# Product of r with state and values as 32 matmuls on four quarters of the array; every PSUM bank handed out by need, and emptied first

## The chip, the cores and the metric

One core of one Trainium2 chip. The metric is the time of one execution in device microseconds. In the trace, PE is TensorE (matmuls), PEld its weight loads, DVE is VectorE, ACT ScalarE, POOL GpSimd and SP the engine that issues most DMAs.

## The reference: a recurrent attention, then a routed expert layer

For each of 4 batches and 8 heads a 40 x 40 state runs over 768 steps, and 3072 tokens of 320 then go through eight experts:

```python
for t in range(S):                                   # S = 768
    y[:, :, t] = einsum('bhd,bhde->bhe', rt, state)
    Sa = einsum('bhde,bhe->bhd', state, at)
    state = state * wt[:, :, None, :] - einsum('bhd,bhe->bhde', Sa, bt) \
          + einsum('bhd,bhe->bhde', vt, kt)
x = y as (3072, 320)                                 # then: score, argmax of 8 experts
out = x + gate * (relu(x @ w1[e]) @ w2[e])           # for tokens whose skip score is > 0
```

All arithmetic is fp32 (the expert products are split into two fp32r parts).

## The kernel before

**Chunks.** The 768 steps are cut into 24 chunks c of 32 steps. The 32 (batch, head) pairs are held as two halves x = 0 and 1; one half's 16 pairs lie on partitions 0 to 39 and 64 to 103. For each chunk and half the work is a chain of small products, each of 16 (or 32) matmuls with 40, 72 or 104 moving columns, with a copy out of PSUM behind each:

- `rs(c,x)`, on even chunks only: r of two chunks (64 columns of `rrt`) with the tile `SV`, which holds the state and the values side by side. One matmul per pair, in two PSUM banks. DVE then multiplies the state rows by `D` into `R1t` (two instructions), ACT copies the value rows into `R1t` (four).
- `ux(c,x)` reads the finished `R1t` block; ACT copies the result to `UX`. `uq(c,x)` multiplies by the inverse in `TB`; four ACT copies put it back into `R1t`, and POOL masks it (`R1t<-R1t,mc`).
- `sst(c,x)` gives the next state: on even chunks 16 matmuls of 72 columns and four ACT copies; on odd chunks two products of 40 columns, one of which ACT copies to `SV`, where the next `rs` reads it.
- `yy(c,0)` and `yy(c,1)` write the outputs of a chunk into one bank (`py`), which DVE empties into `XS` with one multiply. The tile stays in its bank from the first to the second.

Around the chain stand `m1` (products for the inverse, ACT and DVE empty them), `kbt` and `wtt` (transposes), `tinv` (the inverse itself: DVE steps on `px` and `M`, over four chunks), scans on DVE, the routing of finished tokens (`xpose`, `score`, `place`), and DMAs.

**The plan.** From c = 1 to c = 21 no instruction is issued at once. `Rec.call` records each as a task with a cost from `Rec.cost` (one task may be a whole product). At c = 22 `Rec.flush` works out their dependences, gives each task a key (its place in the program less the length of the longest chain of tasks behind it), lets `Rec.plan` place them on the engines by a simulated clock, and issues them in that order. Each engine then works through its own list strictly in order; semaphores hold it where an operand is not ready. All recorded instructions carry one line number in the trace, L230; the others have L117. So groups are told apart by tiles.

**The banks.** The core has eight PSUM banks. Five of them (`pq`, `pc` twice, `ps` twice) are in `rec.banks`: `plan` gives a recorded tile any of these that is free (`ps` only to `ps` tiles and to the oldest tile without a bank), whatever its name in the source. `px` (two) and `py` (one) are outside the pool: `px` serves `tinv`, `py` serves `yy`. In `deps` tasks on different engines that touch a `py` or `px` tile are kept in program order. An instruction that empties a bank has no precedence over others.

`plan` also has a model of TensorE's program fetch: it counts each recorded matmul as four instructions, and lets 256 instructions begin no sooner than 3.6 us after the 256 before.

Of the kernel before, what the change touches and what calls it, by code (L numbers as in the profile page):

```python
# [14 lines left out]
PSUM = bass.MemoryType.PSUM  # L15
# [41 lines left out]
class Rec:  # L57
# [32 lines left out]
    def use(s,ap):  # L90
        n=ap.name
        if 'DRAM' in str(ap.space).upper(): return [(('d',n),15,1)] if n.startswith('xg') else []
        if n[:2] in ('py','px'): n=(n[:2],)
        q,m=s.mask(ap)
        return [(('v',s.own[n]) if n in s.banks else n if isinstance(n,tuple) else ('s',n),q,m)]
    def cost(s,e,op,w,r,a):
        sz=lambda x: int(np.prod([d[1] for d in list(x.ap)[1:]])) if len(list(x.ap))>1 else 1
        n=max(sz(x) for x in (w[:1]+r[:1]))
        if 'dma' in op:
            by=4*n*min(128,w[0].ap[0][1])  # L100
            if 'ind' in op:
                s.ni+=1; return (3.6 if s.ni%2 else 1.05),2.6
            return 0.6,2.2+by/1.7e5
        if e=='P':
            if op=='transpose': return 0.145,0
            o=sz(w[0]); m,k=w[0].ap[0][1],r[0].ap[0][1]
            return (0.03+0.0006*o if m in (40,64) or k==40 and m>64 else 0.04 if k<128 and o<70 else 0.0575 if k<128 else 0.03+0.00026*o),0
        if e=='A': return 0.15+0.00085*n,0
        if e=='G': return (0.08+n*0.0008 if op=='memset' else 0.18 if op=='tensor_copy' else 0.25+0.0021*n),0
        ps=any('PSUM' in str(x.space).upper() for x in w+r)  # L110
        if op=='tensor_tensor_scan': return 0.1+0.00217*n,0
        if op=='transpose': return 0.16+0.00115*n*(1 if n<1000 else 1.4),0
        if op=='memset': return 0.08+0.0003*n,0
        if op=='tensor_tensor': return 0.14+0.00105*n*(1 if ps else 1.6),0
        return 0.16+0.00105*n,0
    def call(s,e,op,fn,a,k):
# [17 lines left out]
    def deps(s):  # L134
        acc={}
        for t in s.tasks: t.p,t.n,t.al=set(),[],set()
        for i,t in enumerate(s.tasks):
            for wr,L in ((0,t.R),(1,t.W)):
                u={}
                for n,q,m in L: u[n,q]=u.get((n,q),0)|m  # L140
                for (n,q),m in u.items():
                    if n[0]=='v': t.al.add(n[1])
                    h=acc.setdefault(n,[])
                    for j,w2,q2,m2 in h:
                        if j!=i and ((wr or w2) and q&q2 and m&m2 or n[0] in ('v','py','px') and s.tasks[j].e!=t.e and (n[0]!='v' or 'P' in (s.tasks[j].e,t.e))): t.p.add(j)
                    if wr and n[0] in 'sd': h[:]=[x for x in h if not (x[0]!=i and x[2]|q==q and x[3]|m==m)]
                    h.append((i,wr,q,m))
        for i,t in enumerate(s.tasks):
            for j in t.p: s.tasks[j].n.append(i)
        for t in reversed(s.tasks):  # L150
            t.up=t.d*s.PW+max([s.tasks[j].up+t.lat+(s.HOP if s.tasks[j].e!=t.e else 0) for j in t.n],default=0)
    def plan(s,keep=False):
# [59 lines left out]
                if not users[o]:  # L212
                    at[bank[o]]=last[o]
        s.st,s.fin,s.bank_of,s.en,s.span=st,fin,bank,en,max(fin)
    LET=1.0; FAR=1.0; ALT=1.0; FILL=None
    def keys(s):

        w=max(sum(t.d for t in s.tasks if t.e==e) for e in 'VAGP')/len(s.tasks)
        s.key=[i*w-s.FAR*t.up for i,t in enumerate(s.tasks)]
    def flush(s):  # L220
        s.on=False
        s.deps(); s.keys(); s.plan()
# [40 lines left out]
def attn(ctx,tc,i,m,out):  # L263
# [3 lines left out]
    rec=m.rec; nc=rec.shim  # L267
# [1 line left out]
    pp=m.pp  # L269
    bk=lambda n,k: [pp.tile([128,512],F32,name=f"{n}{q}") for q in range(k)]  # L270
    PQ,PC,PS,PY,PX=bk("pq",1),bk("pc",2),bk("ps",2),bk("py",1),bk("px",2)
    rec.banks={t.name:t for t in PQ+PC+PS}; rec.rest=[t.name for t in PS]
    ps_c,ps_s,ps_p=(Ring(t,rec) for t in (PC,PS,PQ)); ps_y,ps_x=Ring(PY),Ring(PX); m.ps=ps_p
    V,A,G,TE,SP=nc.vector,nc.scalar,nc.gpsimd,nc.tensor,nc.sync
    NC=4*NPH; NH=2*NPH
    SE=(V,G)[SCAN_POOL]
# [230 lines left out]
    def rs(c,x):  # L507

        if c>=NC or c%2: return
        rr=rrt[c//2].rearrange("p (b h) t -> p b h t",b=2)  # L510
        R=R1[x][c%NR1]; e=slice(eo[x],eo[x]+40); n=(128,104)[x]
        RV=[ps_c.tile([128,8,64],F32,tag="pc",name="psRV") for _ in range(2)]
        with rec.one():
            for hh in range(4):
                for b in (0,2,1,3):
                    s=slice(64*(b//2),64*(b//2)+40); v=(b%2)*4+hh
                    TE.matmul(RV[b//2][0:n,v,:],SV[x][s,v,0:n],rr[s,b%2,2*hh+x,:],start=True,stop=True)
        for bh in range(2):
            V.tensor_tensor(R[e,8*bh:8*bh+8,40:104],RV[bh][e],H[c//2]['D'][e,8*bh:8*bh+8].unsqueeze(2).broadcast_to([40,8,64]),ALU.mult)
        for bh in range(2):  # L520
            A.copy(R[ao[x]:ao[x]+32,8*bh:8*bh+8,40:104],RV[bh][ao[x]:ao[x]+32])
        for bh in range(2):
            A.copy(R1[x][1][ao[x]:ao[x]+32,8*bh:8*bh+8,40:72],RV[bh][uo[x]:uo[x]+32,:,0:32])
        load_vv(c//2+1,x)
# [69 lines left out]
    if 1:  # L594

        with tc.manual_schedule(engines={ET.Pool}):
# [72 lines left out]
            ps_p=r4  # L669
# [488 lines left out]
```

## Time and profile before

| | us |
|---|---|
| median of 3 runs (626.65 to 632.09) | 629.97 |
| the profiled execution, its own time | 625.79 |
| its span, first to last instruction | 624.0 |
| mean granted clock of TensorE, share of full speed | 0.879 |

| busy over the span | us | share |
|---|---|---|
| PE | 504.8 | 81% |
| PEld | 425.0 | 68% |
| DVE | 454.9 | 73% |
| ACT | 365.1 | 59% |
| POOL | 310.5 | 50% |

The shares are averages over stages with different limits; PE is counted busy while any matmul is in flight. One fp32 matmul of the source leaves two MATMUL and two LDWEIGHTS records, so x32 in a row is 16 matmuls of the source. [...] A bracket behind a row gives the idle time of that engine just before it and what released it.

### The profile page before, as it was taken

What the parts mean: (1) busy time and instruction counts of PE and PEld (TensorE: products, weight loads), DVE (VectorE), ACT (ScalarE), POOL (GpSimd) and SP (SyncE); (2) the same over time, 40 slices, a digit from 0 to 9 for tenths busy, and PEclk for the clock granted to TensorE, in tenths of its full rate; (3) what the DMA queues carried; (4) which work ended last, traced back from release to release, by engine and by line L of the source; (5) the groups of instructions that cost most, each with busy time, mean ns of one, the idle gap of its engine ahead of it and who ended that gap; (6) DMA issues with size and microseconds to landing.
All of it is one profiled execution on the core that took longest, in us unless ns stands there. A gap on an engine that the chain in (4) does not pass through costs nothing. (4 is left out here: it accounts for less than half of the span.)

```text
span 624.0 us, 27220 instructions
## 1 busy us (share of the span) xinstructions
PE 504.8 (81%) x11748; PEld 425.0 (68%) x11748; DVE 454.9 (73%) x1088; ACT 365.1 (59%) x858; POOL 310.5 (50%) x225
## 2 busy tenths in 40 slices
PE   5775748787785888778787898888787999999995
PEld 2543437676674776667666686766675699999995
DVE  8998957885888668876868759575463458888871
ACT  6471646665864658556675768577655355554540
POOL 5471874446446754275553913321222156666661
PEclk9686767868995889859798989799867999999998
DMA  7873197235452454335443345443566587766100
GB/s 193 209 195 92 36 211 186 71 86 129 111 144 78 103 148 117 93 86 137 120 121 99 92 111 142 117 109 80 140 158 176 154 228 227 232 220 197 51 27 24
DMA packets 80688, 81.93 MB, mean 131 GB/s; under 512 B 49041, under 2 KB 68062, under 8 KB 80099
## 3 DMA queue, kind: packets, MB, share of 16 engines
q1 hardware_dynamic: 78643, 76.35, 46.2%
q0 software_dynamic: 1920, 3.79, 1.7%
q8 instruction: 94, 1.54, 1.0%
q14 instruction: 31, 0.25, 0.1%
HBM read 62.69 MB, written 13.15 MB: 122 GB/s over the span
## 5 line engine op out<-in xcount | busy, mean ns | idle before, releaser
L230 POOL TENSOR_TENSOR R1t<-R1t,mc 64x512 f32<-64x512 f32 x42 | 60.6, 1444 | 90.4 <-ACT R1t L230 64.3
L230 ACT COPY R1t<-pc 32x288 f32<-32x288 f32 (+4 forms) x155 | 67.1, 435 | 28.7 <-PE pc L230 23.7
L117 POOL TENSOR_TENSOR WL<-WR,WH 128x1280 fp32r<-128x1280 f32 (+1 forms) x21 | 58.0, 2789 | 7.1 <-ACT WH L117 7.0
L230 DVE TENSOR_TENSOR px<-px,M 128x168 f32<-128x168 f32 (+10 forms) x240 | 58.2, 267 | 2.1
L230 DVE TENSOR_TENSOR M<-M,px 128x168 f32<-128x168 f32 (+10 forms) x240 | 55.1, 255 | 2.3
L230 ACT COPY R1t<-ps 40x288 f32<-40x288 f32 (+3 forms) x86 | 37.4, 435 | 23.8 <-PE ps L230 16.2
L230 ACT COPY R1t<-pq 32x512 f32<-32x512 f32 (+3 forms) x84 | 37.4, 445 | 16.8 <-PE pq L230 9.8
L230 POOL TENSOR_TENSOR WR<-WR,M 104x1024 f32<-104x1024 f32 x14 | 34.0, 2441 | 18.4 <-DMA WR<-kb 11.8
L117 ACT CAST WH<-WR 128x1024 fp32r<-128x1024 f32 (+1 forms) x35 | 39.7, 1133 | 0.0
L230 PE MATMUL ps<-R1t,L2t 128*40 128x40 f32 (+1 forms) x800 | 34.0, 238 | 6.6 <-ACT R1t L230 6.4
L117 POOL DMA_INDIRECT out<-ro,ti x16 | 15.7, 982 | 45.6 <-DVE ro L117 10.4
L117 DVE CAST ti<-xe 128x2 int32<-128x2 f32 x8 | 37.4, 4673 | 0.2
L230 DVE TENSOR_TENSOR_SCAN M<-M 104x1041 f32<-104x1041 f32 (+1 forms) x14 | 35.4, 2529 | 0.8 <-ACT WE L230 0.7
L117 ACT ACTIVATE hH<-pc 128x512 fp32r<-128x512 f32 x21 | 12.6, 598 | 39.1 <-PE pc L117 39.1
L230 PEld LDWEIGHTS ps<-R1t,L2t 128*40 128x40 f32 x800 | 27.3, 135 | 11.2 <-ACT R1t L230 8.4
L230 PE MATMUL pc<-rrt,SV 40*104 40x64 f32 (+1 forms) x272 | 29.9, 285 | 5.0 <-DVE base L230 2.3
L117 PE MATMUL pc<-xH,WH 128*128 128x256 f32 x126 | 32.5, 283 | 0.0
L230 PEld LDWEIGHTS pc<-rrt,SV 40*104 40x104 f32 (+1 forms) x272 | 27.9, 197 | 5.8 <-DVE base L230 2.5
L230 POOL TENSOR_TENSOR M<-M,mc 128x256 f32<-128x256 f32 x18 | 16.9, 945 | 30.1 <-DVE M L230 17.6
L230 POOL DMA_INDIRECT xg<-XS,ix x18 | 21.6, 1201 | 19.8 <-DMA xg<-XS,ix 6.2
L117 DVE TENSOR_TENSOR WL<-WR,WH 128x1024 fp32r<-128x1024 f32 (+1 forms) x19 | 23.8, 1254 | 9.7 <-ACT WH L117 9.2
L230 PE MATMUL py<-L2t,R1t 128*32 128x40 f32 x1344 | 23.7, 218 | 7.7 <-DVE XS L230 4.3
(385 smaller groups left out, 1614.7 us busy)
## 6 DMA issues: line engine op xcount, KB each, us to landing
WR<-w SPq DMA_DIRECT2D x16, 640.0 KB
WR<-w SPq DMA_DIRECT2D x16, 512.0 KB
L2t<-SCR SPq DMA_DIRECT2D x40, 160.0 KB
WR<-kb SPq DMA_DIRECT2D x32, 160.0 KB
WR<-w SPq DMA_DIRECT2D x16, 256.0 KB
R1t<-vt SPq DMA_DIRECT2D x48, 80.0 KB
SV<-vv SPq DMA_DIRECT2D x48, 80.0 KB
out<-XS SPq DMA_DIRECT2D x24, 160.0 KB
```

Source lines behind the costliest of these rows:

```text
L117: if not s.on: return fn(*a,**k)
L230: for fn,a,k,own in s.tasks[i].calls: (fn if s.en[i]==s.tasks[i].e else s.nc.vector.tensor_copy)(*[at(x,own) for x in a],**{n:at(x,own) fo ...
```

## The change

Four parts. (1) In `rs`, each matmul is split in two by output rows: one with the 40 stationary columns of the state, one with the 64 that hold the values, each on its own half of the array's columns; the two partition halves of the operands already alternate. So 32 matmuls visit four quarters in turn, where 16 matmuls alternated between two halves. The copies behind them are as before. (2) `px` and `py` join the pool, eight banks in all, and lose the special ordering. (3) A task of an engine other than PE that touches a PSUM tile which PE also uses gets its key lowered by `DRAIN` = 30, so it goes ahead of others on its engine. (4) Other constants in `Rec.cost`.

```diff
     def use(s,ap):
-        if n[:2] in ('py','px'): n=(n[:2],)
-        return [(('v',s.own[n]) if n in s.banks else n if isinstance(n,tuple) else ('s',n),q,m)]
+        return [(('v',s.own[n]) if n in s.banks else ('s',n),q,m)]
     def cost(s,e,op,w,r,a):
-            if op=='transpose': return 0.145,0
+            if op=='transpose': return 0.0014*r[0].ap[0][1],0
-            return (0.03+0.0006*o if m in (40,64) or k==40 and m>64 else 0.04 if k<128 and o<70 else 0.0575 if k<128 else 0.03+0.00026*o),0
-        if e=='A': return 0.15+0.00085*n,0
+            return (0.042 if k==40 and m>=40 else 0.041 if o<17 else 0.036+0.00072*o if m==40 else 0.0146+0.00041*o if m==32 else 0.03+0.00165*o)*1.05,0
+        if e=='A': return (0.95 if op=='activation' and n==512 else 0.38 if n==128 else 0.15+0.00085*n),0
...
-        if op=='transpose': return 0.16+0.00115*n*(1 if n<1000 else 1.4),0
+        if op=='transpose': return 0.16+0.00105*n*(1.7 if 'TB' in w[0].name else 1),0
+        if op=='tensor_tensor' and ps and n>300 and not any('PSUM' in str(x.space).upper() for x in r): return 0.14+0.00177*n,0
...
-                        if j!=i and ((wr or w2) and q&q2 and m&m2 or n[0] in ('v','py','px') and s.tasks[j].e!=t.e and (n[0]!='v' or 'P' in (s.tasks[j].e,t.e))): t.p.add(j)
+                        if j!=i and ((wr or w2) and q&q2 and m&m2 or n[0]=='v' and s.tasks[j].e!=t.e and 'P' in (s.tasks[j].e,t.e)): t.p.add(j)
...
+    DRAIN=30.0
     def keys(s):
-        s.key=[i*w-s.FAR*t.up for i,t in enumerate(s.tasks)]
+        pe=set()
+        for t in s.tasks:
+            if t.e=='P': pe|=t.al
+        s.key=[i*w-s.FAR*t.up-(s.DRAIN if t.e!='P' and t.al&pe else 0) for i,t in enumerate(s.tasks)]
...
-    rec.banks={t.name:t for t in PQ+PC+PS}
-    ps_y,ps_x=Ring(PY),Ring(PX)
+    rec.banks={t.name:t for t in PQ+PC+PS+PX+PY}
+    ps_y,ps_x=Ring(PY,rec),Ring(PX,rec)
...
     def rs(c,x):
-        e=slice(eo[x],eo[x]+40); n=(128,104)[x]
+        e=slice(eo[x],eo[x]+40); g=slice(ao[x],ao[x]+64)
-                    TE.matmul(RV[b//2][0:n,v,:],SV[x][s,v,0:n],rr[s,b%2,2*hh+x,:],start=True,stop=True)
+                    for q in (e,g): TE.matmul(RV[b//2][q,v,:],SV[x][s,v,q],rr[s,b%2,2*hh+x,:],start=True,stop=True)
```

## Rows read from the trace of the kernel before

**Rows 1.** Busy time of each engine in five stages, in us from the span's start: columns are the stage, its length, busy time (x instructions) of each engine, the mean granted clock, the busy share of the DMA engines and their GB/s. The recorded part is 74.3 to 445.

```profile
74.30:88.00 13.70, 2.59 (x133) 2.25 (x132) 6.07 (x9) 2.50 (x10) 10.97 (x15) 0.73 0.69 173
88.00:445.00 357.00, 290.00 (x8734) 243.31 (x8734) 264.94 (x818) 240.28 (x608) 175.70 (x136) 0.88 0.45 115
445.00:480.00 35.00, 26.16 (x738) 22.02 (x730) 17.55 (x35) 19.43 (x51) 8.02 (x7) 0.75 0.60 160
480.00:604.00 124.00, 121.90 (x1000) 115.50 (x990) 95.65 (x133) 60.76 (x89) 71.69 (x35) 0.99 0.57 172
604.00:624.00 20.00, 12.82 (x97) 12.55 (x95) 4.91 (x10) 2.39 (x4) 3.92 (x5) 0.89 0.08 27
```

**Rows 2.** The same table for four stretches of 17.5 us inside the loop.

```profile
192.50:210.00 17.50, 12.74 (x277) 11.03 (x273) 12.76 (x39) 8.94 (x22) 10.04 (x11) 0.59 0.33 90
210.00:227.50 17.50, 15.08 (x558) 12.74 (x554) 11.78 (x15) 10.53 (x29) 12.47 (x11) 1.00 0.59 148
...
262.50:280.00 17.50, 11.78 (x264) 10.29 (x260) 13.87 (x46) 9.81 (x25) 11.86 (x12) 0.61 0.26 73
280.00:297.50 17.50, 15.28 (x524) 12.89 (x522) 10.92 (x18) 11.19 (x31) 9.97 (x10) 1.00 0.53 136
```

**Rows 3.** From the timeline of PE, the twelve longest of its waits in the loop whose releaser read a bank of the kind that the waiting matmul writes: start, length, instruction, count, and the wait in brackets.

```profile
121.56 0.40 PE L230 MATMUL pc<-rrt,SV 40*104 40x64 f32 x1 [2.18 <-DVE TB L230]
...
150.08 0.32 PE L230 MATMUL pq<-rrt,SV 40*128 40x64 f32 x1 [1.36 <-DVE M L230]
...
183.80 0.42 PE L230 MATMUL pc<-WR,L1t 128*32 128x64 f32 x14 [1.33 <-ACT R1t L230]
196.14 0.42 PE L230 MATMUL py<-L2t,R1t 128*32 128x40 f32 x11 [2.88 <-DVE XS L230]
202.31 0.44 PE L230 MATMUL ps<-WR,L1t 128*32 128x64 f32 x8 [1.53 <-ACT R1t L230]
228.82 0.30 PE L230 MATMUL pq<-rrt,SV 40*104 40x64 f32 x1 [1.22 <-DVE M L230]
...
250.04 0.37 PE L230 MATMUL pc<-WR 128*32 128x64 f32 x12 [1.45 <-ACT SCR L230]
257.88 0.43 PE L230 MATMUL ps<-mc,XS 128*128 128x128 f32 x1 [1.93 <-DVE R1t L230]
269.79 0.43 PE L230 MATMUL pc<-rrt,SV 40*104 40x64 f32 x1 [2.30 <-DVE base L230]
274.61 0.44 PE L230 MATMUL ps<-WR 128*32 128x64 f32 x8 [1.10 <-DVE R1t L230]
337.40 0.42 PE L230 MATMUL ps<-WR,L1t 128*32 128x64 f32 x14 [1.08 <-ACT xT L230]
388.78 0.32 PE L230 MATMUL py<-L2t,R1t 128*32 128x40 f32 x13 [1.00 <-DVE XS L230]
```

**Rows 4.** From the table of waits in the loop: who waited for whom, us in total, how often, the longest. "issue" is time in which the engine waited for nothing that the profile shows.

```profile
PE ps L230 <- ACT R1t L230: 9.6, 16, 1.6
PE pc L230 <- issue: 7.9, 9, 2.7
PE pc L230 <- ACT R1t L230: 7.6, 13, 1.3
```

**Rows 5.** All matmuls of r with state and values (instructions that touch `rrt`): in the loop and in the stretch behind it; columns are busy time (x records) of PE and PEld, then clock and DMA.

```profile
88.00:445.00 357.00, 46.41 (x640) 42.48 (x640) 0.88 0.45 115
445.00:480.00 35.00, 5.49 (x64) 5.03 (x64) 0.75 0.60 160
```

**Rows 6.** Bursts of matmuls in the timeline of PE, all at the full clock: start, length from the first record to the end of the last, stationary shape, moving shape, records. The first is r with the values in the prologue (16 matmuls of the source with 32 stationary columns, on four quarters of the array), the second and third the product of the loop for x = 0 and for x = 1 (16 of the source), the fourth a product of `sst` with 40 stationary columns on two column halves (8 of the source).

```profile
31.40 0.65 PE L117 MATMUL pq<-rrt,SV 40*32 40x64 f32 x32
219.24 2.16 PE L230 MATMUL pc<-rrt,SV 40*128 40x64 f32 x32
334.15 1.68 PE L230 MATMUL pc<-rrt,SV 40*104 40x64 f32 x32 [0.23 <-ACT UX L230]
438.07 0.51 PE L230 MATMUL ps<-R1t,L2t 128*40 128x40 f32 x16
```

**Rows 7.** Groups by tile: the state's multiply on DVE and the value copies on ACT that empty the product (x busy us, mean ns), and one of the 128-column copies.

```profile
L230 DVE TENSOR_TENSOR R1t<-pc,D 40x512 f32<-40x512 f32 x17 | 11.7, 691 | 17.7 <-PE pc L230 12.5 <-ACT R1t L230 2.7 <-PE pq L230 2.3
L230 ACT COPY M<-pc 128x128 f32<-128x128 f32 x18 | 6.9, 384 | 4.0 <-PE pc L230 3.7
L230 ACT COPY R1t<-pc 32x512 f32<-32x512 f32 x17 | 9.6, 575 | 11.6 <-PE pc L230 9.4 <-POOL R1t L230 1.4 <-PE pq L230 0.6
L230 ACT COPY R1t<-pc 32x256 f32<-32x256 f32 x17 | 6.0, 363 | 0.9 <-PE py L230 0.6
```

**Rows 8.** DVE's timeline around the wait at 269.79: a scan, and the read of `base`; then the inverse when it is put into `TB`.

```profile
264.37 3.38 DVE L230 TENSOR_TENSOR_SCAN M<-M 104x1040 f32<-104x1040 f32 x1
...
269.58 0.15 DVE L230 TENSOR_TENSOR base<-pc,base 128x8 f32<-128x8 f32 x1
...
280.63 1.98 DVE L230 STREAM_TRANSPOSE TB<-M 128x1024 f32<-128x1024 f32 x1
```

**Rows 9.** PE's timeline where the chunk begins that first reads this inverse.

```profile
298.69 0.36 PE L230 MATMUL pq<-UX,TB 32*32 32x104 f32 x5
```

**Rows 10.** The DMA queues: the one that carries TensorE's program, packets and MB; and PE waits in the timeline that only "issue" ended.

```profile
q8 instruction: 94, 1.54, 1.0%
...
96.03 0.38 PE L230 MATMUL pc<-UX,TB 32*32 32x72 f32 x11 [2.66 <-issue]
...
226.47 0.38 PE L230 MATMUL pc<-UX,TB 32*32 32x104 f32 x7 [0.58 <-issue]
...
296.95 0.39 PE L230 MATMUL pc<-R1t,L1t 128*32 128x104 f32 x8 [1.18 <-issue]
```

## What the change should do to the time

> **What bounds the kernel now.** I read the stages first. Behind 480 us the experts keep TensorE busy for 121.90 of 124 us; the change doesn't touch that. The recorded loop fills 357 us, and there no engine is full: PE 81%, DVE 74%, ACT 67% [rows 1]. So the loop is bound by PE together with what PE waits for. The second view cuts it into equal stretches: two of them execute 558 and 524 matmul records at the full clock, two others only 277 and 264, at a mean granted clock of 0.59 and 0.61 [rows 2]. The slow ones are where PE stood waiting, and where the clock then fell to its lower level. Third, the waits of PE one by one, to see which are for an operand and which for a bank. Twelve have a releaser that was reading a bank of the kind the waiting matmul writes; they sum to 19.4 us [rows 3]. PE's waits for ACT's copies to `R1t` are the largest groups by name, 9.6 and 7.6 us, and part of these are for operands [rows 4]. Last, the product of r itself: 46.41 us of PE in the loop for 20 products (640 records of 32), 2.32 us each, and 5.49 us for the two behind it [rows 5].
>
> **The product of r.** At the full clock one takes 2.16 us for x = 0 and 1.68 us for x = 1 [rows 6]. Both stream 64 columns through 16 matmuls and differ only in their stationary columns, 128 against 104: the ratio of the times is 1.29, that of the columns 1.23. So the loading of the weights sets their pace now, not the streaming. The mean at the full clock is 1.92 us; the 2.32 us measured is 1.21 times that, from products that ran partly at the lower clock or with a wait inside.
>
> The new form, 32 matmuls on four quarters, is not in this trace. Its nearest row has the same `rrt` and `SV`, the same 64 moving columns and four quarters in turn, with 32 stationary columns: 16 matmuls in 0.65 us [rows 6]. Twice that is 1.30 us, one end. The other end: if matmuls that share half the array's rows or columns don't overlap, only two run at a time. The `sst` product with 40 stationary columns on two halves takes 0.51 us for 8, so 32 would take 2.04 us, a loss of 0.12 us against 1.92. I take 1.30, the row that differs least. With the same factor 1.21 this is 1.57 us, and 20 products cost 31.4 in place of 46.41 us: 15.0 us of PE less. If the lower clock goes too it is 46.41 - 26.0 = 20.4; at the bad end 20 x 2.47 = 49.4, 3 us more.
>
> Not all of that reaches the end. What frees PE ahead of a waiting instruction is worth nothing. A product is emptied by two DVE multiplies (691 ns each, 1.4 us) and four ACT copies (2 x 575 and 2 x 363 ns, 1.9 us) [rows 7], unchanged, and `ux` waits for all six. But the product stands on the chain from `SV` to `ux`, and it blocks PE for the other half's work; both speak for a gain. I count half, 7.5 us. Behind the loop two products save 5.49 - 2 x 1.57 = 2.3 us, half of it 1 us.
>
> **The banks.** Three more banks come into the pool, those of `px` for as long as no inverse is in work and `py` when no output is open, and the emptying instruction goes first on its engine. Which of the 19.4 us this removes can be followed at one place. At 269.79 the product waited 2.30 us for DVE to read `base` out of its bank; DVE read it at 269.58, after a scan from 264.37 to 267.75 and a train of steps of the inverse [rows 8]. An instruction under way isn't broken off, so going first would have put the read at 267.75, and 1.8 of 2.3 us go. A free bank would take all of it. At 196.14 and 388.78 `yy` waited 2.88 and 1.00 us for its only bank to be read into `XS` [rows 3]; a second bank takes both. Against it: a matmul let in earlier soon meets the next wait, for ACT's copy of its operand. Of 19.4 us I count 8, some 40%; the ends are 0 and all 19.4.
>
> **What goes first pushes something back.** On DVE that is the inverse, in whose place evacuations now run. It was in `TB` at 282.61 [rows 8], and the first matmul that reads it began at 298.69 [rows 9]: 16 us of cover. I cost the delay at nothing. If the cover were gone, every microsecond would stand on the chain, five times (one inverse for four chunks). `px` as a pooled tile could also hold two banks that the chain needs, but they are the two that it held before. The relaxed order of `px` and `py` adds no instruction.
>
> **The costs in the plan** change no instruction, only the order. The old constant gave the product 16 x 0.0684 = 1.09 us, where the rows have 1.68 and 2.16; a 128-column ACT copy had 0.26 and now has 0.38, where the row has 384 ns [rows 7]. An order planned by nearer costs should wait less, but nothing here prices it. I take zero, with 9.6 us on either side, the whole of the largest wait of PE for ACT in rows 4, as what an order can win or lose.
>
> **Sum.** 7.5 + 1 + 8 = 16.5 us against the profiled execution's own 625.79: 609.3. That execution lies 4.2 us under the median of the runs, 629.97, so the forecast is 613.5, taken as 614.
>
> **Rivals.**
>
> *Everything is gained* (slack on PE is used at once, the clock stays up): 15.0 + 2.3 + 19.4 = 36.7 us, 593; less the scan that can't be broken off and similar remnants, 598. For it: the fast stretches of rows 2 show that the loop can run twice as many matmuls in the same time. Against it: DVE has 265 us of its own work in the loop and ACT 240 [rows 1].
>
> *Emptying takes over.* The product falls below the 1.9 us that ACT needs to empty it, PE then waits for ACT where it waited for the bank, and the gains of both parts shrink to the 1 us behind the loop and some 3 of the banks: 626. For it: PE's waits for ACT's `R1t` copies are the largest groups already [rows 4]. Against it: ACT is at 67%, and a bank can now be had elsewhere. [...]
>
> *The quarters don't overlap*, so the change doesn't do what it says: 3 us lost, 8 gained, 5 in all: 625. The prologue burst speaks against it.
>
> *TensorE's program runs dry, and the kernel is slower.* The split adds 16 matmuls to 22 products, four instructions each: 20 x 64 = 1280 in the loop, on 17468 [rows 1], 7.3%. The program comes in 94 packets [rows 10]; the page counts 23496 matmul and load records, so 250 a packet. The densest stretch has 558 + 554 in 17.5 us [rows 2], 15.7 ns each, 3.9 us a packet. Where PE is at that pace, the time follows the count of instructions and not their length: 1280 x 15.7 ns = 20 us if all of them fell there, 13 if two thirds do, while the shorter product buys nothing; with 3 us from the banks this is 640. It decides where a packet's worth of work takes less than 3.9 us. For it: PE stood still for "issue", which could be such a wait, for 7.9 us [rows 4], once for 2.66 us [rows 10]. Against it: the stretches that hold the slow products run at half the pace. [...]
>
> **How the numbers follow.** The forecast 0.47 (606 to 623), everything gained 0.14 (598), emptying takes over 0.17 (626), no overlap 0.08 (625), program dry 0.14 (640). One per cent of 629.97 is 6.3 us, and that is about what a measurement of this kernel can tell from no change: its three runs lie within 5.4 us. Below 623.7 lie the forecast but for a sliver, and all of the first rival: 0.61. Within one per cent lie the second and third and that sliver: 0.26. Above 636.3 lies most of the last: 0.13. The range leaves out 0.2: half of the first rival, most of the last: 598 to 637.
>
> **What would show it.** The product's matmuls in the loop should sum to 26 to 32 us of PE in place of 46.41, twice as many records, each burst near 1.3 us; 40 or more says that the quarters don't overlap. The `yy` waits for `XS` and the waits of the product for `base` and `M` should be gone, and the clock of the loop above 0.88. Emptying takes over if PE's waits for `R1t` grow by what the bank waits lose. The program runs dry if "issue" grows past 15 us and falls inside bursts. An inverse that reaches `TB` less than a few us before its first reader would make the step on cover wrong; so would an ordering in which PE's waits are as long as now, at other places.

## The result: 609.62 us, and the profile after

| | before | after |
|---|---|---|
| median, us | 631.03 (626.65 to 632.68) | 609.62 (604.67 to 616.53) |
| ratio after / before | | 0.9645, 95% interval 0.9537 to 0.9753 |
| the profiled execution, us | 625.79 | 604.67 |
| its span, us | 624.0 | 602.5 |
| mean granted clock | 0.879 | 0.908 |

The change made the kernel 3.5% faster; 614 was forecast, in a range of 598 to 637. The time is right. Two of the steps that lead to it are not: one gave nothing that the runs can tell, and another gave more than it was counted for.

Some executions are 1.5 to 2.2% longer than the fastest of the same kernel (of the kernel after, one took 616.53 us at a mean granted clock of 0.89, the fastest 604.67 at 0.908); medians in this text are over all executions, while ratios leave such ones out. The kernel before was timed again beside every run (medians of 626.98 to 631.03 us), and a ratio is to that. So kernels are compared by their ratios, of which 1% is some 6.3 us; where only medians are given, the text says so.

From the page of the kernel after: busy time of the engines, and TensorE's program queue (packets, MB, share).

```profile
PE 477.5 (79%) x12452; PEld 397.2 (66%) x12452; DVE 463.2 (77%) x1100; ACT 359.3 (60%) x846; POOL 305.3 (51%) x225
...
q8 instruction: 100, 1.64, 1.2%
```

PE is busy 27 us less than before and has 704 more matmul records; its program has grown by six packets [rows 10]. The stages of the kernel after, as in rows 1 (stage, length, busy time and instructions of PE, PEld, DVE, ACT, POOL, then clock and DMA):

```profile
73.50:86.50 13.00, 1.03 (x46) 0.70 (x35) 5.69 (x7) 2.43 (x8) 10.90 (x14) 0.71 0.63 157
86.50:421.50 335.00, 269.84 (x9398) 220.56 (x9398) 277.42 (x830) 235.35 (x603) 171.88 (x136) 0.92 0.50 129
421.50:460.00 38.50, 24.08 (x806) 19.72 (x803) 18.39 (x37) 20.03 (x53) 8.34 (x7) 0.75 0.53 144
460.00:582.00 122.00, 120.26 (x971) 114.53 (x972) 92.06 (x134) 60.26 (x87) 71.79 (x35) 0.99 0.56 163
```

The same borders in the work lie in the kernel before at 87, 445, 481 and 604 us:

```profile
87.00:445.00 358.00, 291.00 (x8762) 244.14 (x8766) 265.94 (x819) 240.40 (x609) 176.51 (x136) 0.88 0.45 116
445.00:481.00 36.00, 27.16 (x750) 22.77 (x739) 17.61 (x36) 20.37 (x54) 8.02 (x7) 0.75 0.59 157
```

The whole gain is in the recorded loop: 358 to 335 us, 23 less. The stretch behind it is 2.5 us longer. The experts are as before.

The product of r in the loop and behind it, after (the view of rows 5: busy time and records of PE and PEld, clock, DMA):

```profile
86.50:421.50 335.00, 29.34 (x1280) 25.49 (x1280) 0.92 0.50 129
421.50:460.00 38.50, 3.88 (x128) 3.24 (x128) 0.75 0.53 144
```

It takes 29.34 us of PE where it took 46.41 [rows 5]; the forecast was 31.4. The quarters do overlap. One product at the full clock, first and last lines of its burst in PE's timeline, where its records go to two banks by turns:

```profile
329.85 0.27 PE L233 MATMUL px<-rrt,SV 40*40 40x64 f32 x2
...
330.79 0.22 PE L233 MATMUL py<-rrt,SV 40*64 40x64 f32 x1
```

From 329.85 to 331.01 it is 1.16 us, where rows 6 have 2.16 and 1.68 and the forecast had 1.30. But other products of the loop have holes:

```profile
112.66 0.27 PE L233 MATMUL pq<-rrt,SV 40*64 40x64 f32 x1 [0.66 <-issue]
...
248.74 0.27 PE L233 MATMUL px<-rrt,SV 40*40 40x64 f32 x2 [0.45 <-issue]
...
263.20 0.32 PE L233 MATMUL pq<-rrt,SV 40*40 40x64 f32 x3 [0.25 <-issue]
```

In the middle of a burst all operands are there and the banks are open. These waits have no releaser on any engine. The table of PE's waits from 100 to 421 us shows how many there are (who waited for whom: us in total, times, the longest; it starts at 100 us to leave out the wait of some 12 us with which the loop begins in both kernels):

```profile
PE px L233 <- issue: 5.8, 9, 1.2
PE pc L233 <- issue: 5.7, 10, 1.7
PE pq L233 <- issue: 3.8, 8, 0.8
PE py L233 <- issue: 3.2, 4, 2.2
...
PE ps L233 <- issue: 2.4, 5, 1.1
```

They sum to 20.9 us. The same stretch of the kernel before has 6.5:

```profile
PE pc L230 <- issue: 4.5, 6, 1.2
PE pq L230 <- issue: 0.9, 2, 0.5
PE py L230 <- issue: 0.8, 2, 0.6
PE ps L230 <- issue: 0.3, 1, 0.3
```

Waits for ACT's copies to `R1t` went the other way, from 20.1 to 8.0, those for DVE's writes of `R1t` from 8.7 to 4.0, and those for `base` from 2.6 to none. All waits of PE together are 58.3 us after and 58.9 before (62.4 up to the end of its loop at 445): little of the gain is that PE waits less. Bank waits went and "issue" took their place. By the stages above, 21 of the 23 us are busy time of PE (291.00 to 269.84), 17 of them the product; the granted clock of the loop rose from 0.88 to 0.92.

What most of the "issue" waits are can be read from the trace. Number all records of TensorE, its matmuls, its weight loads and the semaphore instructions between them, in order of start, and look for holes of more than 0.15 us from one start to the next. They pile up at one place of each 256 records: before record 193, 449, 705 and so on, the same in both kernels and in the runs below. From 100 us to the end of the loop the kernel after has 71 such places; 28 of them have a hole, 23.1 us in all, while no other place of the 256 has more than 5 holes or 3.9 us. The kernel before has 67 places, 15 holes and 10.5 us. Of the "issue" waits 15.3 of 20.9 us end at such a place after (the one at 112.66 is among them, the other two above are not), and 6.6 of 7.2 before. The program comes in 100 packets for 24904 matmuls and loads, so about 250 a packet, and 26 of the 28 holes end 1.1 to 1.8 us after such a packet has landed. No two packets in the loop begin less than 3.38 us apart (3.26 in the kernel before; the model in `plan` has 3.6). So I read these holes as TensorE waiting for the next block of its program. Below they are called block holes.

### The profile page after: what moved, and what is told of

Its sections match the earlier page's. It is cut to its first block, busy times and chain, and to the rows that moved or that the text cites. A ratio compares the mean times of both kernels' runs of the same rounds, so it can differ in the third digit from the quotient of the medians.

```text
span 602.5 us, 28644 instructions
## 1 busy us (share of the span) xinstructions
PE 477.5 (79%) x12452; PEld 397.2 (66%) x12452; DVE 463.2 (77%) x1100; ACT 359.3 (60%) x846; POOL 305.3 (51%) x225
## 5 line engine op out<-in xcount | busy, mean ns | idle before, releaser
L233 ACT COPY R1t<-pc 32x288 f32<-32x288 f32 (+4 forms) x121 | 52.7, 437 | 20.7 <-PE pc L233 12.5
L233 ACT COPY R1t<-px 32x288 f32<-32x288 f32 (+4 forms) x91 | 40.3, 443 | 16.0 <-PE px L233 6.1
L117 DVE TENSOR_TENSOR WL<-WR,WH 128x1024 fp32r<-128x1024 f32 (+1 forms) x19 | 23.8, 1254 | 12.5 <-ACT WH L117 11.9
L233 POOL DMA_INDIRECT xg<-XS,ix x18 | 18.4, 1022 | 28.1 <-DVE XS L233 16.8
L233 ACT COPY R1t<-py 32x416 f32<-32x416 f32 (+4 forms) x56 | 25.3, 451 | 8.0 <-PE py L233 4.6
L117 PE MATMUL ps<-WH,hH 128*128 128x320 f32 x88 | 27.6, 314 | 0.0
L117 PE MATMUL pc<-xH,WL 128*128 128x256 f32 x126 | 27.3, 281 | 0.0
L117 PE MATMUL ps<-WL,hH 128*128 128x320 f32 x88 | 27.2, 309 | 0.0
L117 PE MATMUL ps<-WH,hL 128*128 128x320 f32 x88 | 27.2, 309 | 0.0
L233 DVE TENSOR_TENSOR pc<-pc,M 128x48 f32<-128x48 f32 (+20 forms) x96 | 25.8, 269 | 1.8
L117 ACT COPY R1t<-pc 32x416 f32<-32x416 f32 (+3 forms) x36 | 15.6, 440 | 18.0 <-DVE R1t L117 11.6
L117 PE MATMUL ps<-mc 128*128 128x512 f32 x34 | 22.8, 778 | 4.4 <-DMA mc<-mc 2.9
```

Source lines behind the costliest of these rows:

```text
L117: if not s.on: return fn(*a,**k)
L233: for fn,a,k,own in s.tasks[i].calls: (fn if s.en[i]==s.tasks[i].e else s.nc.vector.tensor_copy)(*[at(x,own) for x in a],**{n:at(x,own) fo ...
```

## The experiments

The theory behind the forecast had two halves: the shorter product is worth half of its PE time, and the banks with the emptying first are worth a little more than that. The main rival was that TensorE's program cannot follow, so that the time goes by the count of instructions. "Pinned" kernels keep the exact order of issue of the kernel that they are compared with: the edited task is given the cost and the instruction count that the plan had for it, so only what is issued differs.

**The new product alone, in the order of before** (pinned).

```diff
-                    TE.matmul(RV[b//2][0:n,v,:],SV[x][s,v,0:n],rr[s,b%2,2*hh+x,:],start=True,stop=True)
+                    for q in (e,g): TE.matmul(RV[b//2][q,v,:],SV[x][s,v,q],rr[s,b%2,2*hh+x,:],start=True,stop=True)
...
+        rec.pin(0.03+0.0006*64,16,64)
```

> The order, the banks and the precedence of the kernel before (its plan is kept: the product's task keeps its old cost and its old count of instructions), and only the product executes as 32 matmuls on four quarters. Measured so far: before 631.0, after 609.6 us. If the shorter product pays as the prediction counted (half of some 15 to 18 us of PE, and 1 behind the loop): 619 to 624 us, product's PE time in the loop 28 to 32 us in place of 46.4. If the gain came from the order and the banks alone, or the added instructions eat the product's gain: 627 to 632 us, and in the second case PE's issue waits in the loop grow from 10 us by 5 or more.

Measured: 629.14 us, ratio 1.0034 (1.0001 to 1.0067). The product between 88 and 421 us, in the kernel before and in this one (whose profiled execution took 634.73 us):

```profile
88.00:421.00 333.00, 43.96 (x598) 40.30 (x600) 0.87 0.45 116
88.00:421.00 333.00, 29.57 (x1216) 25.15 (x1216) 0.86 0.46 116
```

PE's waits for "issue" rose from 9.1 to 20.8 us (from 100 us on, 6.5 to 18.4). The matmuls are 14 us shorter and the kernel is not: the block holes of the loop rose from 10.5 to 24.7 us, by as much.

**The old product in the order of after** (pinned).

```diff
-                    for q in (e,g): TE.matmul(RV[b//2][q,v,:],SV[x][s,v,q],rr[s,b%2,2*hh+x,:],start=True,stop=True)
+                    TE.matmul(RV[b//2][0:n,v,:],SV[x][s,v,0:n],rr[s,b%2,2*hh+x,:],start=True,stop=True)
...
+        rec.pin(0.042*1.05,32,128)
```

> The converse: order, banks and costs of the kernel after (plan kept), but the product executes as 16 matmuls as before, 1280 instructions fewer in the loop. If the product pays on its own: 617 to 624 us against 609.6. If the program of TensorE is what now binds, the longer product is paid back by fewer issue waits: these fall from 25 us in the loop towards 15, and the time is 606 to 613 us. If order alone made the gain: 609 to 611.

Measured: 605.52 us, ratio 0.9681 (0.9638 to 0.9724): nearly the whole gain without the new product. By the ratios the product is worth 0.4% here, 2 us, and the intervals allow anything from 5 us lost to some 10 gained (an estimate from the two intervals). Its "issue" waits are back at 7.0 us from 100 to 421:

```profile
PE px L238 <- issue: 2.8, 3, 1.4
...
PE pq L238 <- issue: 1.5, 3, 1.0
PE py L238 <- issue: 1.5, 2, 0.8
...
PE pc L238 <- issue: 0.7, 1, 0.7
...
PE ps L238 <- issue: 0.5, 1, 0.5
```

The product runs 41.14 us here against 29.34, 14 us of "issue" have gone, and the block holes are 10.4 us in place of 23.1: in this order, too, what the split saves on PE is about what it adds in holes. In the old order it bought nothing, in its own nothing that these runs can tell.

This run shows one thing more. Its matmuls are those of the kernel before, and its loop is 30 us shorter (358 to 328):

```profile
86.50:414.50 328.00, 273.97 (x8758) 229.35 (x8758) 276.04 (x832) 235.30 (x607) 172.25 (x136) 0.93 0.52 132
```

PE is busy for 273.97 us where the same work took 291.00, at a granted clock of 0.93 in place of 0.88. The granted clock reads 1.0 or 0.5 in the traces (in the kernel before 0.50 from 189.70 to 206.77 us and 1.00 from there to 230.66); 0.5 was granted for 48 us of this loop and for 89 us of the one before. So more than half of what the new order gains in the loop is busy time of PE, which goes with the higher clock, and the rest is time in which PE stood idle. Whether the fewer waits brought the clock up isn't tested.

**No precedence for emptying.**

```diff
-    LET=1.0; FAR=1.0; DRAIN=30.0; ALT=1.0; FILL=None
+    LET=1.0; FAR=1.0; DRAIN=0.0; ALT=1.0; FILL=None
```

> The kernel after with DRAIN = 0: eight banks, new product and new costs, but nothing that empties PSUM goes ahead; the plan is made anew. If the precedence carries a good part of the bank gain: 614 to 622 us, and waits of PE for DVE reads of a bank (base, XS, M) come back above 1 us each. If eight banks are enough without it: 606 to 612.

Measured: 629.02 us, ratio 1.0043 (1.0004 to 1.0082): the gain is gone, 4.0% by the ratios. PE's waits of 100 to 421 us:

```profile
PE pq L233 <- DVE base L233: 10.1, 1, 10.1
PE ps L233 <- DVE R1t L233: 6.9, 5, 1.8
...
PE px L233 <- DVE R1t L233: 5.7, 2, 3.1
...
PE pq L233 <- DVE R1t L233: 2.7, 1, 2.7
```

One wait alone costs 10 us. The timelines of PE and of DVE at that place:

```profile
183.57 0.48 PE L233 MATMUL ps<-rrt,SV 40*40 40x64 f32 x4
194.13 0.37 PE L233 MATMUL pq<-rrt,SV 40*40 40x64 f32 x2 [10.08 <-DVE base L233]
```

```profile
183.23 2.32 DVE L233 TENSOR_TENSOR_SCAN M<-M 104x1041 f32<-104x1041 f32 x1
...
186.43 1.43 DVE L233 TENSOR_SCALAR D<-M 104x16 f32<-104x16 f32 x1
...
188.37 2.31 DVE L233 TENSOR_TENSOR_SCAN M<-M 104x1040 f32<-104x1040 f32 x1
...
193.76 0.24 DVE L233 TENSOR_TENSOR M<-M,px 128x84 f32<-128x84 f32 x1
193.92 0.16 DVE L233 TENSOR_TENSOR base<-pq,base 128x8 f32<-128x8 f32 x1
```

The product stands in its own middle, with its second bank still unread: DVE does two scans and 24 other instructions, most of them steps of the inverse, before the read of `base`, 0.16 us long, that gives the bank back. It is the event of [rows 8], more than four times as long. Eight banks do not help against it: once the plan has given the product that bank, it waits.

**Precedence alone, on the kernel before.**

```diff
-    LET=1.0; FAR=1.0; ALT=1.0; FILL=None
+    LET=1.0; FAR=1.0; DRAIN=30.0; ALT=1.0; FILL=None
     def keys(s):
...
-        s.key=[i*w-s.FAR*t.up for i,t in enumerate(s.tasks)]
+        pe=set()
+        for t in s.tasks:
+            if t.e=='P': pe|=t.al
+        s.key=[i*w-s.FAR*t.up-(s.DRAIN if t.e!='P' and t.al&pe else 0) for i,t in enumerate(s.tasks)]
```

> The kernel before with the one line of precedence (DRAIN = 30), nothing else: five banks by need, old product, old costs. If the precedence alone makes the gain, as the run without it (629.0) suggests: 604 to 614 us, against 627 to 631 for before. If it needs the nearer costs or the three banks: 618 to 630.

Measured: 621.29 us, ratio 0.9877 (0.9832 to 0.9923). Faster by 1.2%, about 7 us by medians: a real part, but not the whole.

**`px` and `py` outside the pool, the rest of the change in place.**

```diff
-    rec.banks={t.name:t for t in PQ+PC+PS+PX+PY}
+    rec.banks={t.name:t for t in PQ+PC+PS}
-    ps_y,ps_x=Ring(PY,rec),Ring(PX,rec)
+    ps_y,ps_x=Ring(PY),Ring(PX)
```

(the last lines shortened; the lines of `use` and `deps` as they were before)

> The kernel after with px and py outside the pool again (five banks by need, old ordering of px and py); product, precedence and costs as after; the plan is made anew. If the three banks carry a good part: 614 to 622 us and yy waits for XS again. If precedence and product make the gain: 606 to 612.

Measured: 609.49 us, ratio 0.9738 (0.9692 to 0.9784). The median is that of the kernel after, but the kernel before was 4 us faster beside this run, and the ratio is 0.9% worse, some 6 us; the two intervals overlap. So with the precedence in place the three banks are worth 6 us at best guess and by these intervals anything from nothing to some 13; the runs don't settle it.

**Precedence and the new costs, five banks, old product.**

```diff
...
+            return (0.042 if k==40 and m>=40 else 0.041 if o<17 else 0.036+0.00072*o if m==40 else 0.0146+0.00041*o if m==32 else 0.03+0.00165*o)*1.05,0
...
+        rec.pin(0.042*1.05,32,64)
```

> The kernel before with the precedence and the new cost constants only (the old product priced at the 1.41 us of after): five banks, old product. If these two parts, which issue no instruction differently, make the whole gain: 602 to 612 us. If the three banks or the product carry some of it: 613 to 622.

Measured: 619.45 us, no ratio: three executions took 619.35 to 620.3 us, one 609.16, so each of the two expectations has its execution. This run decides nothing.

**Instructions against time.** The sharpest question is whether PE in the kernel after is held by the time of its matmuls or by their number. Two kernels keep its order and add work to each of the 20 products in the loop, in front of it and into the same banks, where the product overwrites it; nothing of the computation is left out. One adds 32 tiny matmuls (2560 instructions in all), the other a single one of 320 columns over the full array (80 instructions, 17 us of PE by the trace).

```diff
+            for hh in range(4 if rec.on else 0):
+                for b in (0,2,1,3):
+                    s=slice(64*(b//2),64*(b//2)+40); v=(b%2)*4+hh
+                    for q in (0,64): TE.matmul(RV[b//2][q:q+32,v,0:8],SV[x][s,v,q:q+32],rr[s,b%2,2*hh+x,0:8],start=True,stop=True)
...
+        rec.pin(0.042*1.05,32,128)
```

```diff
+            if rec.on: TE.matmul(RV[0][:,0:5,:],m.tri,m.mc[:,0:320],start=True,stop=True)
...
+        rec.pin(0.042*1.05,32,128)
```

> The plan of the kernel after is kept; each of the 20 recorded products executes 32 further small matmuls ahead of its own (32 stationary, 8 moving columns; their results are overwritten), 2560 instructions in all, some 0.6 us of PE each, 12 in all. If the program is what binds: issue waits grow from 25 to 45 us or more, the time to 625 to 645. If only PE's time counts: 610 to 622, the issue waits as they were.

> The counterpart: the plan of the kernel after is kept; each recorded product has one further matmul of full width with 320 moving columns ahead of it (overwritten as well), four instructions, 0.55 to 0.8 us of PE each, 11 to 16 in all. If the program binds, this time lies in place of issue waits: these fall or stay, and the time is 607 to 616 us. If PE's time binds as such: 616 to 626.

Measured: 644.91 us (ratio 1.0263, 1.0214 to 1.0313) with the tiny matmuls, 607.91 (0.9628, 0.9565 to 0.9692) with the long ones. The long ones cost nothing that can be told: the ratio is that of the kernel after (0.9645) to 0.2%, with some 8 us either way by the two intervals. The tiny ones cost 35 us by medians, 13.8 ns an instruction. "issue" from 100 to 421 us rose to 35.0 us, while it is 17.5 with the long ones. Of the kernel with tiny matmuls, the busy times on its page; its loop, which now ends at 464.5 us (columns as in the stages above); and the product in it, tiny matmuls included:

```profile
PE 515.8 (80%) x13732; PEld 433.7 (67%) x13732; DVE 463.2 (72%) x1100; ACT 359.8 (56%) x846; POOL 302.3 (47%) x225
...
86.50:464.50 378.00, 306.37 (x10678) 256.64 (x10678) 272.18 (x830) 235.73 (x604) 168.14 (x136) 0.83 0.44 114
...
86.50:464.50 378.00, 47.30 (x2560) 41.46 (x2560) 0.83 0.44 114
```

So the 13.8 ns are not the price of the program alone. In this trace the loop is 43 us longer than after (335). Its block holes are 46.2 us where after has 23.1, 23 us more or 9 ns for each added instruction. The product holds PE 18 us longer (29.34 to 47.30). And all other matmuls hold it 19 us longer (240.50 to 259.07), though they are the same: the granted clock of the loop is 0.83 in place of 0.92. That PE time as such is not the price is shown by the long matmuls: they add as much of it (17 us), their block holes are as before (23.0 us), their loop runs at 0.93 and the kernel is no longer. How much of the 35 us is the lower clock, and whether the holes brought it down, these runs don't separate.

The mean pace says less. From 88 to 421 us the kernel with tiny matmuls executes 18842 records of matmuls and loads, the kernel after 18673: 17.7 and 17.8 ns each, and the kernel before comes to 20.4 ns in its loop (358 us by 17528 records, in its row above). But `p_old_order`, with as much "issue", is at 19.0 ns (17566 records), so there is no one pace that all such loops keep.

**Fewer instructions in the order of after** (pinned). In the loop the score products are issued as one matmul each where they were four on quarters, the place products as two where they were eight: 840 instructions less, and longer matmuls.

```diff
-            for q in range(4): nc.tensor.matmul(lg[32*q:32*q+32],xT[:b-a,k,32*q:32*q+32],s.wg[:b-a,k,:],start=k==0,stop=k==2)
+            for q in ((slice(0,128),) if s.rec.on else [slice(32*q,32*q+32) for q in range(4)]): nc.tensor.matmul(lg[q],xT[:b-a,k,q],s.wg[:b-a,k,:],start=k==0,stop=k==2)
...
```

(and the place products likewise)

> The order, banks and costs of the kernel after (plan kept); only the routing in the loop is written with full-width matmuls: score as 3 in place of 12, the two products of place as 1 in place of 4 each. Some 840 instructions fewer on TensorE in the loop (of some 18800), its busy time about the same. So far: after 609.6, the same order with the old product 605.5 us, PE's issue waits in the loop 25 and 8.5 us. If these waits are TensorE's program arriving late: they fall from 25 us to between 8 and 17, and the time is 598 to 606 us. If they are something that the split product does on the array: unchanged at 23 to 27 us, and 607 to 612.

Measured: 599.84 us, ratio 0.9539 (0.9498 to 0.958). "issue" from 100 us on fell from 20.9 to 10.9. The score and place products take 9 us more of PE (10.87 to 18.52 and 1.66 to 3.16 us between 88 and 421), and the kernel is some 10 us faster by medians, 7 by the ratios; the intervals overlap. It is the trade of the change's product, run backwards, but the block holes fell by less than that (23.1 to 16.6 us), so the trade alone doesn't explain a gain.

**The same routing with the old product** (pinned; beside the lines of `fewer_instr`).

```diff
-                    for q in (e,g): TE.matmul(RV[b//2][q,v,:],SV[x][s,v,q],rr[s,b%2,2*hh+x,:],start=True,stop=True)
+                    TE.matmul(RV[b//2][0:n,v,:],SV[x][s,v,0:n],rr[s,b%2,2*hh+x,:],start=True,stop=True)
```

> The plan of the kernel after with the old product and with the routing in full-width matmuls: some 2100 instructions fewer on TensorE than after. The old product alone gave 605.5, the routing alone 599.8 us. If the program still binds with the routing alone (issue waits 15.7 us there): the old product costs nothing or gains again, 594 to 602 us. If the program has stopped binding, the product's shorter time shows at last: 603 to 610 us here against 599.8.

Measured: 606.98 us, ratio 0.963 (0.9558 to 0.9702); "issue" 4.8 us. Here fewer instructions bring nothing that can be told (605.52 us and 0.9681 without them), and there were only 10.4 us of block holes to be had (7.0 are left). And beside `fewer_instr` the new product is now worth 7 us by medians (599.84 against 606.98), about what the forecast counted; the two intervals just overlap, so the 7 is not firm.

**The old costs in the plan, all else of the change kept.**

```diff
-            return (0.042 if k==40 and m>=40 else 0.041 if o<17 else 0.036+0.00072*o if m==40 else 0.0146+0.00041*o if m==32 else 0.03+0.00165*o)*1.05,0
+            return (0.03+0.0006*o if m in (40,64) or k==40 and m>64 else 0.04 if k<128 and o<70 else 0.0575 if k<128 else 0.03+0.00026*o),0
...
+        rec.pin(0.03+0.0006*64,16,128)
```

> The kernel after with the cost constants of before (the product priced at 1.09 us, as it was): precedence, eight banks and the new product stay, the plan is made anew. Precedence alone on the kernel before gave 621.3 us, all but precedence 629.0, all together 609.6. If precedence needs the nearer costs: 617 to 625. If the banks or the product are what it needs: 606 to 613.

Measured: 596.22 us, ratio 0.9526 (0.946 to 0.9592). The fourth part of the change is worth nothing here. By medians it cost 13 us in this combination, by the ratios 1.2%, some 7 us; the interval overlaps that of the kernel after, so that it cost anything isn't shown.

**Old costs and fewer instructions** (pinned to the order of `old_costs`).

```diff
+        s.rec.pins([0.03+0.00026*9]*8+[0.04]*4,48)
...
+        s.rec.pin(0.03+0.00026*n*8,8,32)
```

(with the score and place products as in `fewer_instr`)

> The order of old_costs (596.22 us, ratio 0.9526), kept as it is, with the score and place products of the loop issued as one matmul each where they were four or eight; the computation is whole. If TensorE's program still holds the loop in that order (its issue waits were 22.4 us there, and in the other order the same removal of instructions gave 609.6 to 599.8), the time falls by 5 to 12 us: 584 to 591, ratio 0.935 to 0.946, issue waits down to some 13 to 16 us. If the order of old_costs had already got rid of what the program costs, the longer score and place products (some 9 us of PE) stand against a few stalls: 594 to 599, ratio near 0.953.

Measured: 596.88 us, ratio 0.9512 (0.9456 to 0.9569); "issue" from 88 us on 15.9, from 22.4. The first of the two expectations failed: fewer program waits, the same time. So 19 us of "issue" in a profile (from 100 us on; 12.5 with fewer instructions) are not 19 us to be had. By the trace the block holes fell by 8 us (24.3 to 16.3), while the score and place products hold PE 11 us longer (11.96 to 23.20 between 88 and 421): the longer matmuls took back what they gave.

| product | costs | routing | us | ratio, interval | block holes, us |
|---|---|---|---|---|---|
| new | new | as is (the change) | 609.62 | 0.9645 (0.9537 to 0.9753) | 23.1 |
| old | new | as is | 605.52 | 0.9681 (0.9638 to 0.9724) | 10.4 |
| new | new | fewer | 599.84 | 0.9539 (0.9498 to 0.958) | 16.6 |
| old | new | fewer | 606.98 | 0.963 (0.9558 to 0.9702) | 7.0 |
| new | old | as is | 596.22 | 0.9526 (0.946 to 0.9592) | 24.3 |
| new | old | fewer | 596.88 | 0.9512 (0.9456 to 0.9569) | 16.3 |

All six have the precedence and eight banks. By medians the other five all lie under the kernel after, three of them by 10 to 13 us; by the ratios four do, by 0.2 to 1.3%, and the interval of each overlaps that of the kernel after. The block holes follow the count of instructions; the times don't follow the block holes alone.

## Why the prediction was right, and where its steps were not

**The size of the product: right.** 31.4 us of PE was forecast for the loop, 29.34 came; 1.30 us a burst, 1.16 came. The nearest row, the four-quarter product of the prologue [rows 6], was a good stand-in.

**The value of the product: wrong.** The step counted half of the 15 us as lying on the path, 7.5. Alone in the old order it gave none (ratio 1.0034), and taken out of the change it is missed by 2 us, where the interval still has room for 7.5. What failed is the assumption that PE time taken off a busy chain turns into time. A product now issues 128 instructions where it issued 64, and the block holes rise by about what PE saves: by 14.2 us against 14.4 in the old order (`p_old_order`), by 12.7 against 11.8 in the new one (`p_undo`). The burst from 329.85 to 330.79 starts its instructions 7.3 ns apart, while the packets of the program begin at least 3.38 us apart, 13 ns for each of 256. As I read it, the new product outruns its program there, and the old one, 64 instructions in 1.9 us, 30 ns each, does not; no run shows the fetch itself.

**The rival of the program: its mechanism was there, its end was not.** The mark that the prediction set, "issue" past 15 us and inside bursts, was met with 20.9 us, and 15.3 us of them end at the place of the block holes, where I read them as waits for the program. Its 640 us did not come because the loss stays about as large as what the product saves, and because the banks gave more than the 3 us allowed there. The chance of 0.14 belonged to the sign of the whole; the mechanism deserved more. The argument against it, that the stretches with the slow products run at half the pace, misread the rows: the product at 219.24 [rows 6] lies in the densest stretch of rows 2, from 210 to 227.5 us. And the holes stand inside the new bursts themselves, which run far above any mean. Two figures fit a program that comes in blocks: 2560 instructions added make 10 packets more (110 against 100), and the holes stand at one place of every 256 records. Of the 71 such places in the loop after, 43 have no hole above 0.15 us; the other 28 cost 23.1 us.

**The banks: under-sized, and the wrong half named first.** 8 us were counted for pool and precedence together. The precedence carries it: without it the whole gain is lost (609.62 to 629.02 us by medians, 4.0% by the ratios), alone it gives 7 us on the old kernel, and what the pool of eight adds can't be told from nothing (0.9738 without it, against 0.9645). The prediction followed one wait of 2.30 us for the read of `base` [rows 8] and put 1.8 of it down to the precedence; that reading of the mechanism was right. It was scaled by the twelve waits in the old trace, 19.4 us [rows 3], but those are the waits of an order planned around the old keys. The same rule in a new order meets other waits: the one in `no_drain` was 10 us. How the 2% between `drain_only` (0.9877) and `p_undo` (0.9681), some 12 us, divide between the pool and the costs stays open: `drain_costs`, which could have told, decided nothing. Each of these kernels is a new order throughout, so the parts need not add.

**The waits named as marks.** Those of the product for `base` are gone, as forecast. Those for `XS` are not: 4.3 us before, 4.9 after, now under `px`, `pq` and `pc`; likewise those for `M`, 4.3 and 4.9. A pool moves a wait to whoever gets the bank; it removes it only if a bank is free. The clock of the loop, forecast above 0.88, was 0.92.

**The inverse at nothing: right.** No wait of PE in the loop after names `TB`; before there were 2.2 us. The inverse is in its place at much the same times: the five transposes began between 133.78 and 414.75 us before, between 137.46 and 406.94 after.

**The costs at zero, within 9.6 us: not refuted.** With the old ones the median is 596.22, 13 us lower and outside the bounds; by the ratios it is some 7 us, inside them, and not clear of the noise. That nearer costs make an order that waits less is not what these runs show. The bound came from the largest wait in the old trace; a new order is not held by it.

**Behind the loop: wrong in sign, and small.** The product saved 1.6 us of PE (5.49 to 3.88), yet the stretch is 2.5 us longer. In PE's timeline, and then in POOL's:

```profile
427.74 0.76 PE L117 MATMUL py<-L2t,R1t 128*32 128x40 f32 x32 [6.18 <-POOL R1t L233]
```

```profile
419.79 0.97 POOL L117 DMA_INDIRECT xg<-XS,ix  x1 [1.74 <-DMA xg<-XS,ix]
426.43 1.26 POOL L233 TENSOR_TENSOR R1t<-R1t,mc 64x512 f32<-64x512 f32 x1 [5.67 <-DMA xg<-XS,ix]
```

On POOL's list the mask of the last chunk stood behind a scatter. The scatter had waited 1.74 us for a DMA; the mask began 5.67 us after the scatter's end, released by another DMA of `xg`. Why the scatter came first isn't shown. The old product in the same order (`p_undo`) has the same wait of 6.0 us. So what was late there was not the product.

**The other rivals.** Emptying did not take over: waits for ACT's `R1t` fell from 20.1 to 8.0 us. What mattered was which bank is emptied first: without the precedence one wait for a bank was 10.08 us. The quarters overlap: 32 matmuls took 1.16 us where 16 had taken 1.68 and 2.16 [rows 6]. Everything gained, 598, was reached by no part of the change, but by `old_costs` and `old_costs_fewer`, by their medians.

So 614 was near 609.62 by luck: an over-sized term (8.5 us for the product) and an under-sized one (8 us for the banks, where the order of the change with the old product gains 3.2%, about 20 us) made up for each other.

## What to carry to other kernels

Splitting a matmul trades PE time for instructions. Before it is priced, number the records of TensorE and look for holes at one place of every 256, as these traces have them. Where a loop has them, and "issue" waits stand inside its bursts, the added instructions can cost what the shorter matmul saves, as they did here in two orders; joining small matmuls is then worth a try, though here it brought 7 to 10 us at best in one order and nothing in another. Where a planner hands out banks, let what empties a bank go ahead of the rest on its engine before adding banks: a read of 0.16 us behind a train of scans held PE for 10 us, with eight banks in the pool. Judge an order by the granted clock, too: the same matmuls took 17 us less of PE in the order that had it at 0.93 in place of 0.88. And do not add up parts of a re-planned schedule: take each out alone and in the order of the others, since the order moved this kernel by more than the change of the arithmetic did.

## What the runs showed of the hardware that was not expected

TensorE started the 128 instructions of one product within 0.94 us (from 329.85 to 330.79, after), but in the loops of these kernels no two packets of its program began less than 3.26 us apart (`before`; 3.30 to 3.49 in the thirteen others). With one packet for about 250 of its instructions, that is some 13 ns each at best (an estimate, 3.26 us by 250). In the kernel after, 18 of the 71 blocks of 256 records from 100 us on ran in under 3.3 us, and 17 of these were followed by a hole of more than 0.15 us; of the 53 slower ones 11 were. These are the 28 block holes, 23.1 us; 26 of them end 1.1 to 1.8 us after a packet has landed. With 2560 tiny matmuls and loads added there are 37, 46.2 us. Added full-array matmuls of 17 us cost nothing that could be told in such a loop, while the 2560 tiny instructions, with as much PE time (18 us), cost 35 us, in a loop with a granted clock of 0.83.
